# Reciprocal denominators sent through DRAM instead of through TensorE, and a border between two layers put in another order

## The chip, the cores and the metric

The kernel runs on one NeuronCore of a Trainium2 chip. The metric is the device time of one execution in microseconds; the number that counts is the median of several runs.

## What is computed

Four layers over 2048 tokens of width 576: linear attention, MLP, linear attention, MLP, each with a residual. The same weights serve both layers of a kind.

```python
def _A_ref(x, wqkv, wo):                       # 32 heads of 18
    q, k, v = split_heads(x @ wqkv)
    phi = lambda t: jnp.where(t > 0, t + 1, jnp.exp(t)) + 1e-6
    pq, pk = phi(q), phi(k)
    kv  = jnp.einsum("bhsd,bhse->bhde", pk, v)
    z   = jnp.einsum("bhsd->bhd", pk)
    num = jnp.einsum("bhqd,bhde->bhqe", pq, kv)
    den = jnp.einsum("bhqd,bhd->bhq", pq, z)[..., None] + 1e-6
    return merge_heads(num / den) @ wo

def _B_ref(x, w1, b1, w2, b2):                 # 576 -> 4608 -> 576
    h = gelu(_layernorm(x) @ w1 + b1)
    return h @ w2 + b2

x = x + _A_ref(_layernorm(x)); x = x + _B_ref(_layernorm(x))   # twice over
```

The output is x, in bfloat16.

## The kernel before

**Attention.** For each of 16 token tiles of 128 the kernel makes k and v, and adds up `kv` over all tokens in one PSUM pair (`kvacc`). The q products are made in 20 pieces (`q_proj`): five groups of seven heads (126 rows, the last of four heads and 72 rows) times four blocks of 512 tokens. Nine of them stand among the token tiles, eleven in the border. phi(q) of a piece lies in a `units` buffer; its second half on VectorE (`finish`, two instructions) can be done later.

After the last tile, `kv` is multiplied with `wo` once (`kv_wo`), so that the output of a tile of 128 tokens (`wo_stage`) is ten matmuls of 288 columns, five groups by two halves, plus an addition to x on VectorE. Before that, phi(q) has to be divided by the denominators. `den_stage(c)` makes the denominators of one block of 512 tokens in PSUM (32 heads by 128 tokens, four times), takes the reciprocal (`rden`), and lays it out with a mask. `scale_stage(g, c)` then spreads the 32 head rows over the 126 rows of a group with a matmul against a 0/1 matrix (`head_bc`, 512 columns, result in `rden_ps`), and VectorE multiplies phi(q) by it.

**The border.** The MLP's first block needs only the first four token tiles. So the kernel starts its first product while blocks 2 to 4 of the attention are still to be scaled and multiplied out. A first-product group (`m1_group`, four units of 128 hidden rows, 512 tokens) is 36 matmuls that use only 64 rows of TensorE each, upper and lower half side by side, so two run at a time; each half of a unit must finish before the other half begins on the same PSUM bank, and a tiny ScalarE copy (`relay`) carries that order. ScalarE then evicts each unit with gelu; the fourth eviction of a group (`held`) is put behind the next group's relay, or, in the border, flushed at once. Eight groups stand in the border and a ninth in `run`, then the second product (`m_ps`) begins. All instructions of an engine run in the order in which the source issues them (`InOrder`, `pe`).

**PSUM.** Two pairs of banks (`accA`, `accB`) are used in turn by groups, `wo_stage`, `kv_wo` and the second product; four single banks (`one`) go round among everything else. A group takes two singles and one pair: units 0 and 2 lie in the singles, units 1 and 3 in the pair. Evictions go 0, 2, 1, 3.

**The first border, in TensorE's order:** the last q products, `den_stage(0)` and the five scalings of block 1 (three read PSUM directly, two go over a ScalarE copy); four times a `wo_stage` with the next layer's norm, q products and transposes of the norm's output between them, `den_stage(1)` after the second; then

```python
            scales(1, 0, 1); finish(4); group()
            scales(1, 2, 3); finish(1); den_stage(2); group()
            scales(1, 4);    finish(4); group()
            for c in (1, 2, 3):          # wo_stage, one scaling, wo_stage, one scaling, group,
                ...                      # twice per block; den_stage(3) in block c == 1
```

The border of the second attention layer is written by the same code.

Of the kernel before, what the change touches and what calls it, by code (L numbers as in the profile page):

```python
# [15 lines left out]
P = 128  # L16
# [4 lines left out]
G = 5  # L21
# [14 lines left out]
def build(tc, A_x, A_wqkv, A_wo, B_w1, B_b1, B_w2, B_b2, out, n_layers=4):  # L36
    nc = tc.nc
    with ExitStack() as ctx:
# [3 lines left out]
        work = ctx.enter_context(tc.tile_pool(name="work", bufs=2))  # L42

# [124 lines left out]
        relay_sb = const.tile([P, 2], F32, name="relay_sb")  # L168
        pool.memset(relay_sb[:], 0.0)
# [102 lines left out]
        class Norm:  # L272
# [32 lines left out]
            def norm(self):  # L305
# [10 lines left out]
                if self.kind == "B":  # L316
                    pool.tensor_copy(out=y[:, D:DPAD], in_=y[:, 4 * P:D])
# [84 lines left out]
        def layer_A(li, next_kind, begin, before_tile, mid_tile, rows_ahead, after_tile, q_tiles, placed, mlp):  # L402
# [155 lines left out]
            quad_rden, turn = {}, dict(rb=0)  # L558

            def spare(i):  # L560

                return yT[:, i, CA:2 * CA]

            def den_stage(c):
# [9 lines left out]
                quad = spare(3 + c % 2)  # L574
                vec.tensor_tensor(out=quad.rearrange("p (j n) -> p j n", j=4), in0=quad_mask[:],
                                  in1=rden[:].unsqueeze(1).to_broadcast([P, 4, P]), op=ALU.mult)
                quad_rden[c] = quad

            def scale_stage(g, c, direct=False):
                bp = one("rden_ps")  # L580
                mm(bp[:], head_bc[:, g, :], quad_rden[c], True, True)
                if direct:
                    vec.tensor_tensor(out=pq[(g, c)][0:GR[g], 0:CA], in0=bp[0:GR[g], :],
                                      in1=pq[(g, c)][0:GR[g], 0:CA], op=ALU.mult)
                    return
                turn["rb"] += 1
                rb = spare(turn["rb"] % 3)
                act.copy(out=rb[0:GR[g], :], in_=bp[0:GR[g], :])
                vec.tensor_tensor(out=pq[(g, c)][0:GR[g], 0:CA], in0=pq[(g, c)][0:GR[g], 0:CA],
                                  in1=rb[0:GR[g], :], op=ALU.mult)  # L590
# [11 lines left out]
            first = [Norm(t, "B", "act" if t < 3 else "dve", "act" if t < 2 else "dve") for t in range(TPC)]  # L602
# [26 lines left out]
            q_next(True)  # L629
            first[2].transposed()  # L630
            q_next(True)
            first[3].transposed()
            warm_table(ACT.Gelu_apprx_tanh)
# [3 lines left out]
            def scales(c, *groups):  # L637
                for g in groups:
                    scale_stage(g, c, direct=True)

            def group():
                mlp.m1_group(0, mlp.done)
                mlp.flush()

            scales(1, 0, 1)
            finish(4)
            group()
            scales(1, 2, 3)
            finish(1)
            den_stage(2)  # L650
            group()
            scales(1, 4)
            finish(4)
            group()
            for c in (1, 2, 3):
                t = c * TPC
                nxt = scales if c < 3 else lambda *a: None
                wo_stage(t)
                nxt(c + 1, 0)
                wo_stage(t + 1)  # L660
                nxt(c + 1, 1)
                group()
                wo_stage(t + 2)
                nxt(c + 1, 2)
                wo_stage(t + 3)
                nxt(c + 1, 3, 4)
                if c == 1:
                    den_stage(3)
                if c < 3:
                    group()  # L670
# [4 lines left out]
        class LayerB:  # L675
# [4 lines left out]
            def m1_group(self, c, g):  # L680
# [5 lines left out]
                dst = [early[0][:], late[:, 0, :], early[1][:], late[:, 1, :]]  # L686
# [29 lines left out]
                for i, (hi, n, wt, mv) in enumerate(order):  # L716
# [11 lines left out]
                    if seen[n] == 9 and n != 3:  # L728
                        evict(n)
# [8 lines left out]
            def run(self):  # L738
# [6 lines left out]
                for c in range(NCB):  # L745
# [15 lines left out]
                    for j in range(TPC):  # L761
                        t = c * TPC + j
                        acc = pair("m2_ps")
                        if t == NT - 1 and li == n_layers - 1:
                            for half in range(2):
                                cols = slice(half * HALF, (half + 1) * HALF)
                                for f in range(NF):
                                    mm(acc[:, half, 0:HALF], hT[f][:, j * P:(j + 1) * P], w2_sb[:, f, cols],
                                       f == 0, f == NF - 1)
                                vec.tensor_tensor(out=x_sb[:, t, cols], in0=acc[:, half, 0:HALF],  # L770
                                                  in1=xo_of[t][:, cols], op=ALU.add)
                                sp.dma_start(out=out_f[t * P:(t + 1) * P, cols], in_=x_sb[:, t, cols])
                            break
                        for f in range(NF):
# [145 lines left out]
```

## Time and profile before

| | us |
|---|---|
| median of 3 runs | 778.02 (778.01 to 778.48) |
| profiled execution, its own time | 777.94 |
| span of its profile | 776.2 |
| TensorE busy | 767.1 |
| ScalarE busy | 315.8 |
| VectorE busy | 274.3 |

The span is the time between the first and the last instruction; the profiled execution's own time has 1.7 us around it. A row of the timeline reads: start, length, engine, line, operation, output and inputs, shapes, count, and in brackets the idle time before it with what ended it. A row's length for a matmul is longer than the step to the next matmul, since they overlap; steps are read from start times. PE is TensorE, PEld its weight loads, DVE is VectorE, ACT ScalarE, POOL GpSimd, SPq the queue on which SyncE issues DMAs.

### The profile page before, as it was taken

Reading aid. Unit: us, or ns where it says so; the run is one execution under the profiler, and the core shown is the slowest. Engines: PE = TensorE matmul, PEld = TensorE weight load, DVE = VectorE, ACT = ScalarE, POOL = GpSimd, SP = SyncE. Lnnn points to the kernel's source line nnn. Section 1 sums busy time; section 2 is a strip of 40 time slices with the busy share of each in tenths; the row PEclk is TensorE's granted clock in tenths of the full one; section 3 lists DMA queues with packets and bytes.
Section 4 is the critical chain, followed back from the end, with each engine's and each line's share of the span. In section 5 each row is a group of like instructions: output and inputs, shape, how many; then the busy total and the mean of one; then the engine's idle time right before and its main releaser. Section 6 shows DMA issues by size and latency. Waiting matters only on the chain.

```text
span 776.2 us, 15424 instructions
## 1 busy us (share of the span) xinstructions
PE 767.1 (99%) x6559; PEld 488.2 (63%) x6580; DVE 274.3 (35%) x636; ACT 315.8 (41%) x657; POOL 113.1 (15%) x238
## 2 busy tenths in 40 slices
PE   8999999999999999999999999999999999999998
PEld 5776555675477457646777754557745764675476
DVE  7876753435223402400354576443130240100000
ACT  5677744204710660274046586331075027305700
POOL 4540200223112201200200020003120120010010
PEclk9999999999999999999999999999999999999999
DMA  8990000010001101010000000000100100010000
GB/s 210 246 352 12 1 1 2 1 35 24 14 11 25 36 1 35 6 30 3 1 17 19 1 3 1 1 2 21 40 7 1 45 21 2 8 50 10 1 16 16
DMA packets 51086, 25.69 MB, mean 33 GB/s; under 512 B 35146, under 2 KB 51018, under 8 KB 51018
## 3 DMA queue, kind: packets, MB, share of 16 engines
q1 hardware_dynamic: 51018, 24.71, 11.8%
q8 instruction: 51, 0.84, 0.5%
q14 instruction: 17, 0.14, 0.1%
HBM read 15.79 MB, written 2.36 MB: 23 GB/s over the span
## 4 chain that ended last, share of the span: by engine, by line
PE 91%; ACT 4%; DVE 3%; issue 1%; POOL 0%; DMA 0%; DVEq 0%; POOLq 0%
PE m_ps L181 36%; PE h_ps L181 19%; PE hp_ps L181 15%; PE v_ps L181 5%; PE k_ps L181 5%; PE q_ps L181 4%; ACT units L52 3%; PE wo_ps L181 3%; PE kvacc L181 1%; DVE units L52 1%; PE rden_ps L181 1%; DVE x_sb L52 1%; DVE ln_st L52 1%; PE tp L330 1%; PE kvwo_ps L181 0%
## 5 line engine op out<-in xcount | busy, mean ns | idle before, releaser
L181 PEld LDWEIGHTS <-units 128*128 128x128 bf16 (+2 forms) x2624 | 254.5, 98 | 76.6 <-issue 11.7
L181 PE MATMUL m_ps<-w_sb,units 128*128 128x288 bf16 x2304 | 283.8, 286 | 0.6 <-DVE x_sb L52 0.6
L181 PEld LDWEIGHTS <-w_sb 64*128 64x128 bf16 x2304 | 124.6, 94 | 138.1 <-issue 7.7
L181 PE MATMUL hp_ps<-yT,w_sb 64*128 64x512 bf16 x1152 | 175.7, 376 | 0.0
L181 PE MATMUL h_ps<-yT,w_sb 64*128 64x512 bf16 x1152 | 151.1, 376 | 1.0 <-DVE units L52 0.6
L52 ACT COPY relay_sb<-relay_sb 128x1 f32<-128x1 f32 x144 | 27.5, 191 | 289.4 <-PE h_ps L181 268.0
L52 DVE TENSOR_TENSOR x_sb<-m_ps,xo 128x576 bf16<-128x576 f32 (+1 forms) x33 | 24.4, 739 | 323.1 <-PE m_ps L181 323.1
L52 ACT ACTIVATE units<-h_ps,b1T 128x512 bf16<-128x512 f32 x144 | 91.2, 684 | 44.5 <-PE h_ps L181 43.2
L52 POOL TENSOR_TENSOR xo<-x_sb,b_bc 128x576 f32<-128x576 bf16 x32 | 40.8, 1275 | 416.5 <-DVE x_sb L52 298.0
L52 ACT ACTIVATE units<-hp_ps,b1T 128x512 bf16<-128x512 f32 x144 | 96.2, 688 | 0.0
L181 PEld LDWEIGHTS <-yT 128*128 128x128 bf16 x640 | 60.8, 97 | 18.7 <-ACT yT L52 1.1
L181 PE MATMUL h_ps<-yT,w_tail 64*128 64x512 bf16 x144 | 54.1, 376 | 0.0
L181 PE MATMUL hp_ps<-yT,w_tail 64*128 64x512 bf16 x144 | 54.1, 376 | 0.0
L52 DVE BATCH_NORM_STATS2 ln_st<-x_sb 128x6 f32<-128x288 bf16 x128 | 51.2, 441 | 1.3 <-DMA x_sb<-in_A_x_dram 0.9
L52 ACT ACTIVATE units<-q_ps 128x512 bf16<-128x512 f32 x80 | 43.4, 602 | 15.7 <-PE q_ps L181 10.9
L181 PE MATMUL q_ps<-yT,wq_sb 128*128 128x512 bf16 x185 | 47.4, 379 | 0.8
L52 DVE STREAM_TRANSPOSE shared<-y_ring 128x640 bf16<-128x640 bf16 x40 | 33.0, 828 | 42.4 <-DMA yT<-shared 40.7
L181 PE MATMUL wo_ps<-shared,units 126*128 126x288 bf16 (+1 forms) x320 | 44.9, 286 | 1.0
L181 PE MATMUL k_ps<-wkv_sb,yT 128*128 128x288 bf16 x320 | 44.6, 286 | 0.2 <-ACT yT L52 0.2
L181 PE MATMUL v_ps<-wkv_sb,yT 128*128 128x252 bf16 (+1 forms) x320 | 44.6, 285 | 0.0
L52 DVE TENSOR_TENSOR x_sb<-wo_ps,x_sb 128x576 bf16<-128x576 f32 x32 | 24.2, 757 | 52.0 <-PE wo_ps L181 50.9
L52 DVE TENSOR_SCALAR y_ring<-x_sb,ln_mv,ln_rstd 128x576 bf16<-128x576 bf16 x58 | 30.7, 529 | 28.2 <-POOL ln_rstd L52 28.2
(69 smaller groups left out, 401.5 us busy)
## 6 DMA issues: line engine op xcount, KB each, us to landing
yT<-shared SPq DMA_DIRECT2D x160, 40.0 KB, 1.9
w_sb<-in_B_w_dram SPq DMA_DIRECT2D x12, 432.0 KB, 8.5
w_sb<-in_B_w_dram SPq DMA_DIRECT2D x9, 512.0 KB, 9.4
x_sb<-in_A_x_dram SPq DMA_DIRECT2D x16, 144.0 KB, 3.3
out_dram<-x_sb SPq DMA_DIRECT2D x15, 144.0 KB, 1.7
wkv_sb<-in_A_wqkv_dram SPq DMA_DIRECT2D x2, 288.0 KB, 3.3
w_tail<-in_B_w_dram SPq DMA_DIRECT2D x2, 288.0 KB, 11.5
wo_sb<-in_A_wo_dram SPq DMA_DIRECT2D x1, 567.0 KB
```

The lines of the kernel that those rows point to most:

```text
L52: inst = issue(*args, **kw)
L181: return pe(nc.tensor.matmul(out_, lhsT=lhsT, rhs=rhs, start=start, stop=stop, **kw))
L330: pe(nc.tensor.transpose(out=tp[:, k, :], in_=self.y[:, k * P:(k + 1) * P], identity=ident[:]))
```

## The change

1. Block 1 is scaled as before, with all five scalings reading PSUM directly. For blocks 2 to 4, `den_stage` ends with four DMAs that write the reciprocals to DRAM as 32 rows of 512, and `spread(c)` reads them back with five DMAs, each head's row 18 times over, into a free part of `yT` (`spare(g)`). `scale_stage` then multiplies two buffers of SBUF on VectorE, without a matmul.
2. The border is written in another order: groups stand in runs of 3, 2, 2 and 1 (the ninth follows the last), with the four `wo_stage` of a block together between them. All nine late finishes come before the first group. `den_stage(1)` moves behind the last transpose. In the first part, a q product goes between the third and fourth scaling, and the norms, q products and transposes are rearranged.
3. In a group, units 0 and 2 lie in the pair and units 1 and 3 in the singles; the eviction of unit 0 is issued when both 0 and 2 are complete. The order of evictions is the same, 0, 2, 1, 3.
4. The last tile's second product takes a single bank for each half instead of one pair. The copies of three transposes instead of two go to VectorE, and so does the small tail copy of the norm of tile 3.

```diff
+        dpool = ctx.enter_context(tc.tile_pool(name="dram", bufs=1, space=DRAM))
...
+        rden_rows = [dpool.tile([H, CA], BF16, name=f"rden_rows{c}") for c in range(NCA)]
...
             def den_stage(c):
...
-                rden = work.tile([P, P], BF16, name="rden", bufs=1)
+                rden = work.tile([P, P], BF16, name="rden", bufs=2)
                     vec.reciprocal(out=rden[:], in_=dp[:, 0:P])
+                if c > 0:
+                    for j in range(TPC):
+                        sp.dma_start(out=rden_rows[c][:, j * P:(j + 1) * P], in_=rden[32 * j:32 * (j + 1), :])
+                    return
...
+            def spread(c):
+                for g in range(G):
+                    sp.dma_start(out=spare(g)[0:GR[g], :],
+                                 in_=rden_rows[c][7 * g:7 * g + GH[g], :].unsqueeze(1).to_broadcast([GH[g], DH, CA]))
+
+            def scale_stage(g, c):
+                rows = slice(0, GR[g])
+                if c > 0:
+                    by = spare(g)
+                else:
+                    by = one("rden_ps")
+                    mm(by[:], head_bc[:, g, :], quad_rden, True, True)
+                vec.tensor_tensor(out=pq[(g, c)][rows, :], in0=by[rows, :], in1=pq[(g, c)][rows, :], op=ALU.mult)
...
-            for g in range(G):
-                if g == 3:
-                    kv_wo(4, act)
-                scale_stage(g, 0, direct=g < 3)
+            for g in range(3):
+                scale_stage(g, 0)
+            kv_wo(4, act)
+            q_next(True)
+            scale_stage(3, 0)
+            scale_stage(4, 0)
             q_next(True)
             for t in range(TPC):
                 wo_stage(t)
-                if t >= 1:
+                if t in (1, 2):
                     first[t - 1].norm()
                 first[t].stats()
                 first[t].rstd()
-                q_next(True)
-                if t >= 2:
-                    first[t - 2].transposed()
-                if t == 1:
-                    den_stage(1)
+                if t < 2:
+                    q_next(True)
+                if t == 2:
+                    first[0].transposed()
+            q_next(True)
+            first[2].norm()
+            first[1].transposed()
+            q_next(True)
+            q_next(True)
             first[3].norm()
...
             first[2].transposed()
             first[3].transposed()
+            den_stage(1)
+            spread(1)
             warm_table(ACT.Gelu_apprx_tanh)
...
+            def groups(n):
+                for _ in range(n):
+                    mlp.m1_group(0, mlp.done)
+                    mlp.flush()
...
+            finish(9)
+            scales(1)
+            groups(3)
+            for t in range(TPC, 2 * TPC):
+                wo_stage(t)
+                if t < TPC + 2:
+                    den_stage(t - 2)
+            spread(2)
+            scales(2)
+            spread(3)
+            groups(2)
+            outputs(2)
+            scales(3)
+            groups(2)
+            outputs(3)
+            groups(1)
...
-                dst = [early[0][:], late[:, 0, :], early[1][:], late[:, 1, :]]
+                dst = [late[:, 0, :], early[0][:], late[:, 1, :], early[1][:]]
...
-                    if seen[n] == 9 and n != 3:
-                        evict(n)
+                    if n in (0, 2) and seen[0] == seen[2] == 9:
+                        evict(0)
+                        evict(2)
+                    if n == 1 and seen[1] == 9:
+                        evict(1)
...
                         if t == NT - 1 and li == n_layers - 1:
                             for half in range(2):
                                 cols = slice(half * HALF, (half + 1) * HALF)
+                                acc = one("m2_ps")
                                 for f in range(NF):
-                                    mm(acc[:, half, 0:HALF], hT[f][:, j * P:(j + 1) * P], w2_sb[:, f, cols],
+                                    mm(acc[:, 0:HALF], hT[f][:, j * P:(j + 1) * P], w2_sb[:, f, cols],
                                        f == 0, f == NF - 1)
```

More of the change, by code (lines that the diff above doesn't have):

```diff
@@ L316, in norm @@
                 if self.kind == "B":
-                    pool.tensor_copy(out=y[:, D:DPAD], in_=y[:, 4 * P:D])
+                    (vec if self.eng == "dve" and self.transpose != "dma" else pool).tensor_copy(out=y[:, D:DPAD], in_=y[:, 4 * P:D])
             def transposed(self):
@@ L599, in wo_stage @@
                 residual(li, t, wp[:, :, 0:HALF])
-            first = [Norm(t, "B", "act" if t < 3 else "dve", "act" if t < 2 else "dve") for t in range(TPC)]
+            first = [Norm(t, "B", "act" if t < 3 else "dve", "act" if t == 0 else "dve") for t in range(TPC)]
             finish(1)
@@ L648, in layer_A, with scales @@
[L648 to L657, printed above, removed]
-                wo_stage(t)
[L659 to L670, printed above, removed]
+            def scales(c):
+                for g in range(G):
+                    scale_stage(g, c)
@@ L773, in run @@
                             break
+                        acc = pair("m2_ps")
                         for f in range(NF):
```

34 lines of the change are left out of this document (5 added, 29 removed).

## Prediction, made before the changed kernel was run

> **What bounds the kernel now.** First the page: busy shares, the granted clock, the chain that ended last.
>
> ```profile
> PE 767.1 (99%) x6559; PEld 488.2 (63%) x6580; DVE 274.3 (35%) x636; ACT 315.8 (41%) x657; POOL 113.1 (15%) x238
> ...
> PEclk9999999999999999999999999999999999999999
> ...
> PE 91%; ACT 4%; DVE 3%; issue 1%; POOL 0%; DMA 0%; DVEq 0%; POOLq 0%
> ```
>
> TensorE is the bound and its clock is whole, so time comes only out of matmuls that go away and of stretches in which TensorE holds an instruction back. A busy share of 99% hides such stretches, because the ends of matmuls are modelled; they are found by start times against paces. The chain of waits gives the paces, from stretches in which nothing disturbs:
>
> ```profile
> 66.48 1.08 PE q_ps L181 x5
> ...
> 93.26 0.40 PE den_ps L181 x20
> ...
> 145.45 35.39 PE m_ps L181 x288
> ...
> 184.83 1.08 PE h_ps L181 x9
> 188.71 1.08 PE h_ps L181 x9
> ...
> 446.51 1.08 PE q_ps L181 x5
> ...
> 525.48 35.39 PE m_ps L181 x288
> ```
>
> A matmul of 512 columns takes 1.08/5 = 0.216 us, one of 288 columns 35.39/288 = 0.123 (so the ten of a `wo_stage` 1.23), a `den_stage` 0.40, and a first-product group in a row of such groups 188.71 - 184.83 = 3.88. The q product at 66.48 and the second product at 145.45 come again at 446.51 and 525.48, both 380.03 us later: the border of the second attention layer is that of the first over again, and what holds for one is counted twice.
>
> Then the timeline of the first border, TensorE's rows and two that bear on them:
>
> ```profile
> 71.34 0.81 PE L181 MATMUL rden_ps<-yT,head_bc 128*128 128x512 bf16 x3
> ...
> 84.31 0.44 PE L330 MATMUL tp<-ident,y_ring 128*128 128x128 bf16 x5
> ...
> 84.59 1.24 PE L181 MATMUL q_ps<-yT,wq_sb 128*128 128x512 bf16 x5
> ...
> 87.49 0.59 PE L181 MATMUL rden_ps<-yT,head_bc 128*128 128x512 bf16 x2
> 87.69 0.49 DVE L52 COPY yT<-tp 128x640 bf16<-128x640 bf16 x1 [0.51 <-PE tp L330]
> ...
> 88.23 1.46 PE L181 MATMUL h_ps<-yT,w_sb 64*128 64x512 bf16 x8
> ...
> 92.65 0.60 PE L181 MATMUL rden_ps<-yT,head_bc 128*128 128x512 bf16 x2
> ...
> 97.80 0.39 PE L181 MATMUL rden_ps<-yT,head_bc 128*128 128x512 bf16 x1
> ...
> 98.12 1.04 PE L181 MATMUL h_ps<-yT,w_sb 64*128 64x512 bf16 x8
> ...
> 108.18 1.26 ACT L52 ACTIVATE units<-h_ps,b1T 128x512 bf16<-128x512 f32 x2 [0.62 <-PE h_ps L181]
> ...
> 109.14 2.89 PE L181 MATMUL wo_ps<-shared,units 126*128 126x288 bf16 x20
> ...
> 112.80 0.39 PE L181 MATMUL h_ps<-yT,w_sb 64*128 64x512 bf16 x1
> 113.48 1.02 PE L181 MATMUL h_ps<-yT,w_sb 64*128 64x512 bf16 x7 [0.29 <-DVE units L52]
> ...
> 117.46 1.41 PE L181 MATMUL wo_ps<-shared,units 126*128 126x288 bf16 x10
> ...
> 131.75 2.90 PE L181 MATMUL wo_ps<-shared,units 126*128 126x288 bf16 x20
> ...
> 134.57 1.04 PE L181 MATMUL h_ps<-yT,w_sb 64*128 64x512 bf16 x8
> ...
> 138.56 2.89 PE L181 MATMUL wo_ps<-shared,units 126*128 126x288 bf16 x20
> ...
> 141.39 1.04 PE L181 MATMUL h_ps<-yT,w_sb 64*128 64x512 bf16 x8
> ...
> 145.38 4.83 PE L181 MATMUL m_ps<-w_sb,units 128*128 128x288 bf16 x38
> ```
>
> I split the border at 87.49, where the last transpose has left TensorE. From there to the second product at 145.38 lie 57.89 us. Work by paces: nine groups 34.92, twelve `wo_stage` 14.76, fifteen spreading matmuls (`rden_ps`) 3.24, two `den_stage` 0.80: 53.72. So 4.2 us are lost, and the rows say where. A group that stands alone costs more than 3.88: from the spreading matmul at 97.80 to the group at 98.12 there are 0.32 where 0.216 would do, and the group from 141.39 to 145.38 takes 3.99: 0.1 to enter and 0.1 to leave the row-tiled state, nine times: 1.8. The first group takes 92.65 - 88.23 = 4.42, 0.43 over 3.99, and begins 0.2 after its turn, for VectorE's copy of the last transpose at 87.69: 0.6. The one at 112.80 takes 4.66, held by VectorE's scaling: 0.7. Two `wo_stage` at 131.75 and 138.56 take 2.82 and 2.83 to the next group where 2.46 + 0.1 would do, 0.26 each; the pair of banks is still being emptied. That is 3.6 of 4.2; the rest is scattered.
>
> **The change, part by part.**
>
> *Spreading matmuls.* Blocks 2 to 4 lose 15 matmuls of 0.216: 3.2 per layer.
>
> *Groups left undisturbed.* The runs of groups become 3, 2, 2 and 2 (the eighth, and the ninth that always followed): four entries and exits instead of nine, 5 x 0.2 = 1.0. Against it: each group is flushed at its end, so its fourth eviction stands ahead of the next group's relay on ScalarE. Two evictions in a row take 1.26 (the row at 108.18), so four end some 2.5 us after the first begins. That is 0.9 before its group ends (109.14 less 0.1, against 108.18); the next group's second halves need the relay half a group in, 1.94 after that end, so 2.8 after the first eviction began. It is just enough: 0 to 0.2 for each of five joints, and I take 0.
>
> *Bank order.* Units 0 and 2, evicted first, now lie in the pair, so the pair is free for `wo_stage` about 1.2 us earlier, more than the 0.26 that it was late. With the scalings no longer between groups the waits at 112.80 go too. The first group's wait stays in part: it needs the copy of the last transpose, about 0.7 after that leaves TensorE, and only `den_stage(1)` of 0.4, moved there, fills it: 0.3.
>
> Second part after: 34.92 + 4 x 0.2 + 14.76 + three `den_stage` 1.20 + 0.3 = 52.0, against 57.89: 5.9 less.
>
> *First part, 71.34 to 87.49.* 16.15 us hold five spreading matmuls 1.08, two `kvwo` 0.25, seven q products 7.56, four `wo_stage` 4.92, `den_stage(1)` 0.40, and four transposes of 84.59 - 84.31 = 0.28: 15.33, so 0.8 is lost. The change takes `den_stage` out (0.4) and puts a q product between the third and fourth scaling, which leaves VectorE room; scaling straight out of PSUM replaces a ScalarE copy and a VectorE product. Between none and all of the 0.8 goes; I take half, 0.4. Together 0.8. One transpose more, and the tail of tile 3's norm, go to VectorE, beside q products.
>
> *The end.* The last tile's second half waits for the first half's addition, since both lie in one pair; now each half has a bank of its own:
>
> ```profile
> 768.45 4.57 PE L181 MATMUL m_ps<-w_sb,units 128*128 128x288 bf16 x36 [0.62 <-DVE x_sb L52]
> ```
>
> 0.6 less, once. The steady groups of blocks 2 to 4 evict in the same order at the same times and keep 3.88.
>
> Sum: 2 x (5.9 + 0.8) + 0.6 = 14.0. The profiled execution took 777.94 (span 776.2 and 1.7 around it), 0.08 under the median 778.02; 777.94 - 14.0 = 763.9, and the difference to the median is below what I resolve.
>
> **What must be hidden.** The scaling of a block now waits for DMA: four writes to DRAM, then five reads that depend on them, all on SP. Nothing in the trace does this, so I bound it:
>
> ```profile
> out_dram<-x_sb SPq DMA_DIRECT2D x15, 144.0 KB, 1.7
> ...
> L52 SPq DMA_DIRECT2D yT<-shared x16: 586/602/1165, 186.2 to 196.6; - x16
> ...
> L52 SPq DMA_DIRECT2D x_sb<-in_A_x_dram x16: 384/431/1613, 0.8 to 18.2; - x16
> ...
> DMA to landing us min/median/max: 2.2/3.3/3.8
> ...
> DMA packets 1925, 2.13 MB, mean 354 GB/s; under 512 B 79, under 2 KB 1925, under 8 KB 1925
> ```
>
> and VectorE's part of the chain, from the groups by form:
>
> ```profile
> L52 DVE TENSOR_TENSOR x_sb<-wo_ps,x_sb 128x576 bf16<-128x576 f32 x32 | 24.2, 757 | 52.0 <-PE wo_ps L181 50.9
> ...
> L52 DVE TENSOR_TENSOR units<-units 128x512 bf16<-128x512 bf16 x40 | 17.0, 426 | 3.8 <-DVE units L52 0.5 <-ACT units L52 0.4
> ...
> L52 DVE TENSOR_SCALAR units<-units 128x512 bf16<-128x512 bf16 x40 | 12.1, 301 | 0.8 <-ACT units L52 0.8
> ...
> L52 DVE RECIPROCAL rden<-den_ps 128x128 bf16<-128x128 f32 x8 | 7.5, 939 | 1.1 <-PE den_ps L181 1.1
> ```
>
> A write lands 1.7 us after issue (stores of the output), a read 2.2 at best (loads of x), a write's issue takes about 0.4. Let s be the time by which each read follows the one before. Its floor is the issue, 0.43 to 0.60. Its ceiling is all 126 rows on one of 16 DMA engines: at 354/16 = 22 GB/s (the loads of the second weight, 46 to 52 us) a row of 1024 bytes takes 0.046, 126 of them 5.8. I take 0.6, by the yT row, whose transfers have the most pieces.
> [...]
>
> Count from the start of the first group. The reciprocal ends at about 0.8, the last write lands at 3.75, the reads are issued from 3.8 and land from 6.0 to 6.0 + 4s, and the last scaling (0.43, VectorE) ends at 6.4 + 4s; the first product that uses it stands at 12.45, after three groups: there is time while s is under 1.5. VectorE first does nine finishes (9 x 0.73 = 6.6), ready at 7.4, ahead of the scaling and not behind it (a finish is 0.301 + 0.426). Block 3: `wo_stage` 4 ends at 13.2, then addition 0.76 and reciprocal 0.94 on VectorE; reads wait on SP behind the writes of block 4 as well, to 18.3, and land up to 20.5 + 4s, 0.43 before they are scaled; needed at 26.2: s under 1.3. Block 4: its reads wait till block 3's scalings have read the buffer, and are needed at 39.1: s under 2.0. Queued behind a late scaling on VectorE are only additions of later `wo_stage`; on SP only later spreads.
>
> **Rivals.** (1) Reads somewhat late: s from 1.3 to 2.2. Above 1.5 a layer loses what blocks 2 and 3 come late by, (4s - 6.05) + (4s - 5.3) = 8s - 11.35; at 1.8, 3.05, twice, so 770.0. For it: nothing in the trace reads the same DRAM row 18 times. Against: at 0.6, or twice that, nothing is lost. (2) Slower: the spread transfers land on too few DMA engines. It decides where that loss eats the gain of a layer, 8s - 11.35 = 6.7, at s = 2.26. On two engines s = 63 x 0.046 = 2.9; then block 4's chain governs, 20.9 + 9s + (4s - 6.05) against 39.1, a loss of 13.4 a layer: 763.9 + 26.9 = 790.8. For it: seven source heads are an odd number to share out. Against: it takes fewer than three of 16. (3) Joints stall 0.2 each: 10 x 0.2 = 2.0, so 765.9.
>
> **How the numbers follow.** Forecast 763.9, with the undecided terms (first part 0 to 0.8 a layer, joints 0 to 2.0, the scattered rest) from 761.5 to 766.5, rival 3 in it: 0.77. Rival 1: 0.12. Rival 2: 0.09. Something between, near 778: 0.02. The range 761.5 to 771 takes the forecast and the cheaper part of rival 1. A measurement tells 0.2%, 1.6 us, from no change: faster 0.88, same 0.02, slower 0.10.
>
> **What would show it.** In the profile after: no `rden_ps` beyond the five of each layer's block 1; groups 3.88 apart in runs of 3, 2, 2 and 2; `m_ps` about 6.7 us earlier; PE rows of `wo_ps` after a run waiting for nothing. Wrong it is if `wo_ps` or its weight load waits for VectorE's `units` or that for `yT<-rden_rows`: then the reads' landing times, and their spacing s above all, say which rival. If the runs of groups have a period over 3.95, the joints stall.

## The result, and the profile after

The changed kernel takes 764.38 us (median of four runs, 764.16 to 765.92) against 778.01 before in the same comparison (four runs, 778.00 to 778.48): a ratio of 0.9828, 95% interval 0.9811 to 0.9845, so 13.6 us or 1.7% less. The forecast was 763.9. The profiled execution took 764.59, with a span of 762.9.

From the page of the kernel after, the rows that answer to the first ones shown of before:

```profile
PE 756.7 (99%) x6550; PEld 485.9 (64%) x6550; DVE 267.1 (35%) x634; ACT 311.7 (41%) x651; POOL 112.5 (15%) x236
...
PEclk9999999999999999999999999999999999999999
...
PE 97%; DVE 1%; DMA 1%; SPq 0%; POOL 0%; issue 0%
```

TensorE is busy 10.4 us less, at the same clock. The chain that ended last now runs over TensorE for 97% of the span, where ScalarE and VectorE had 7% of it. The new DMA path has less than 1% of it: the page names the load of x at the start (`x_sb<-in_A_x_dram`) as its 1% of DMA.

The chain of waits of after, at the places by which the borders were measured before:

```profile
66.83 1.08 PE q_ps L183 x5
...
139.52 5.50 PE m_ps L183 x44
```

```profile
440.57 1.08 PE q_ps L183 x5
...
473.33 1.34 PE wo_ps L183 x10
...
513.07 6.97 PE m_ps L183 x56
```

From the q product to the second product the first border takes 72.69 us and the second 72.50, where both took 78.97: 6.28 and 6.47 less: the second product comes earlier by nearly the 6.7 that the forecast had. The rest of the 13.3 us between the two spans is 0.9 behind the second border (from 513.07 to the end of the span 249.8, from 525.48 before 250.7), less 0.35 by which the q product of the first layer starts later (66.83 against 66.48), ahead of anything that the change touches.

TensorE's rows of the first border, from the timeline:

```profile
71.69 0.81 PE L183 MATMUL rden_ps<-yT,head_bc 128*128 128x512 bf16 x3
...
86.99 0.47 PE L183 MATMUL den_ps<-units,zsel 127*32 127x128 bf16 x20
...
87.76 1.04 PE L183 MATMUL hp_ps<-yT,w_sb 64*128 64x512 bf16 x8 [0.30 <-DVE yT L53]
...
99.52 1.41 PE L183 MATMUL wo_ps<-shared,units 126*128 126x288 bf16 x10
...
113.44 5.29 PE L183 MATMUL wo_ps<-shared,units 126*128 126x288 bf16 x40
...
118.66 1.04 PE L183 MATMUL hp_ps<-yT,w_sb 64*128 64x512 bf16 x8
...
126.54 5.10 PE L183 MATMUL wo_ps<-shared,units 126*128 126x288 bf16 x40
...
139.45 6.79 PE L183 MATMUL m_ps<-w_sb,units 128*128 128x288 bf16 x54
```

Three groups lie between 87.76 and 99.52, 11.76 us: three times 3.88 and 0.12 at the end of the run. Between 118.66 and 126.54 lie two, 7.88, which is two times 3.88 and the same 0.12. No joint stalls, and the first group waits 0.30, as forecast. The four `wo_stage` of block 4 follow one another in 131.57 - 126.54 = 5.03 (the next group starts at 131.57), those of block 3 in 118.66 - 113.44 = 5.22. That 0.19 is the only place where the DMA path holds TensorE up, and SP's and VectorE's rows say how:

```profile
88.60 3.06 SPq L53 DMA_DIRECT2D rden_rows<-rden  x4
92.82 4.13 SPq L53 DMA_DIRECT2D yT<-rden_rows  x5
102.61 3.89 SPq L53 DMA_DIRECT2D rden_rows<-rden  x8
106.67 8.25 SPq L53 DMA_DIRECT2D yT<-rden_rows  x10
```

```profile
95.86 0.43 DVE L53 TENSOR_TENSOR units<-yT,units 126x512 bf16<-126x512 bf16 x1 [0.74 <-DMA yT<-rden_rows]
...
99.48 0.42 DVE L53 TENSOR_TENSOR units<-yT,units 72x512 bf16<-72x512 bf16 x1 [0.31 <-DMA yT<-rden_rows]
...
109.78 0.43 DVE L53 TENSOR_TENSOR units<-yT,units 126x512 bf16<-126x512 bf16 x1 [3.36 <-DMA yT<-rden_rows]
...
113.64 0.42 DVE L53 TENSOR_TENSOR units<-yT,units 72x512 bf16<-72x512 bf16 x1 [0.36 <-DMA yT<-rden_rows]
```

Each first row of a block is the first scaling, each second the last. A scaling starts when its read has landed. The last scaling is needed by the fifth matmul of the block's first `wo_stage`, 4 x 0.123 = 0.49 after that stage's start: at 100.01 for block 2, at 113.93 for block 3. It ends at 99.90 and at 114.06. So block 2 is in time by 0.1 us and block 3 late by 0.1, where the forecast saw 3.6 and 2.9 us to spare. In the second layer block 2 has 1.4 us to spare (its last scaling ends at 472.33 and is needed at 473.75) and block 3 again 0.1 (487.57 and 487.66); block 4 is scaled by 121.19, 5 us ahead of its stage at 126.54. The gain is the one forecast; the margin under it is almost gone.

### The profile page after: what moved, and what is told of

Its sections match the earlier page's. It is cut to its first block, busy times and chain, and to the rows that moved or that the text cites. A ratio compares the mean times of both kernels' runs of the same rounds, so it can differ in the third digit from the quotient of the medians.

```text
span 762.9 us, 15463 instructions
## 1 busy us (share of the span) xinstructions
PE 756.7 (99%) x6550; PEld 485.9 (64%) x6550; DVE 267.1 (35%) x634; ACT 311.7 (41%) x651; POOL 112.5 (15%) x236
## 4 chain that ended last, share of the span: by engine, by line
PE 97%; DVE 1%; DMA 1%; SPq 0%; POOL 0%; issue 0%
PE m_ps L183 37%; PE hp_ps L183 20%; PE h_ps L183 16%; PE q_ps L183 6%; PE wo_ps L183 5%; PE v_ps L183 5%; PE k_ps L183 5%; PE kvacc L183 1%; PE tp L332 1%; DMA x_sb<-in_A_x_dram 1%; SPq L53 0%; PE den_ps L183 0%; PE kvwo_ps L183 0%; DVE yT L53 0%; DVE ln_st L53 0%; DVE units L53 0%
## 5 line engine op out<-in xcount | busy, mean ns | idle before, releaser
L183 PE MATMUL h_ps<-yT,w_sb 64*128 64x512 bf16 x1152 | 177.8, 376 | 0.0
L183 PE MATMUL hp_ps<-yT,w_sb 64*128 64x512 bf16 x1152 | 148.2, 376 | 0.6 <-DVE yT L53 0.6
L53 ACT ACTIVATE units<-hp_ps,b1T 128x512 bf16<-128x512 f32 x144 | 91.2, 684 | 58.8 <-PE hp_ps L183 58.8
L53 ACT ACTIVATE units<-h_ps,b1T 128x512 bf16<-128x512 f32 x144 | 96.2, 688 | 0.0
L183 PE MATMUL q_ps<-yT,wq_sb 128*128 128x512 bf16 x200 | 49.4, 379 | 0.2
L183 PE MATMUL wo_ps<-shared,units 126*128 126x288 bf16 (+1 forms) x320 | 42.6, 286 | 0.0
L53 ACT ACTIVATE phi_e<-k_ps 128x288 bf16<-128x288 f32 x64 | 24.6, 418 | 38.5 <-PE k_ps L183 36.8
```

The lines of the kernel that those rows point to most:

```text
L53: inst = issue(*args, **kw)
L183: return pe(nc.tensor.matmul(out_, lhsT=lhsT, rhs=rhs, start=start, stop=stop, **kw))
```

## The experiments

**Theory:** the parts add up. The spreading matmuls are worth their own time, each group that no longer stands alone 0.2, the banks and the tail the waits they end; the DMA path costs nothing as long as its reads are in time. **Rivals:** the order alone carries the gain and the path through DRAM little; the path through DRAM does what the spread on TensorE did, at a price that is hidden only by luck; the transfers' time is set not by the number of DMA engines but by their issue.

### The parts, one by one

The kernel before with the new banks and the last tile's single banks alone:

```diff
-                dst = [early[0][:], late[:, 0, :], early[1][:], late[:, 1, :]]
+                dst = [late[:, 0, :], early[0][:], late[:, 1, :], early[1][:]]
...    # and the eviction condition and the last tile's second product, as in the change
```

> Kernel before with only the new bank order and the single banks of the last tile. Theory 1: the last tile's 0.6 us, two waits of 0.26 us a layer ahead of output tiles, and the smaller ones of 0.08 (four a layer): 778.0 - 0.6 - 2 x 0.8 = 775.8 (774.5 to 777). Theory 2, the bank order needs the runs to be of use: only the 0.6, 777.4.

Measured: 774.64 (774.54 to 774.65), ratio 0.9956 (0.9939 to 0.9972), 3.4 us less than before. By the chains of waits its two borders take 77.72 and 77.71 us where before takes 78.97, 1.25 less each, and 0.7 go behind the second border. The forecast had named only two waits for the pair of banks, 0.26 each, but the timeline of before has one at five of the six pairs of output stages. The first of them:

```profile
102.11 2.90 PE L181 MATMUL wo_ps<-shared,units 126*128 126x288 bf16 x20
...
104.84 0.38 PE L181 MATMUL rden_ps<-yT,head_bc 128*128 128x512 bf16 x1
```

These twenty matmuls take 2.73 where 2.46 would do; only the pair at 117.46 has no such wait.

The order, banks and tail of after, but the spread of blocks 2 to 4 on TensorE; block 2's five spreads stand ahead of the first run of groups, those of blocks 3 and 4 between the output stages:

```diff
             def scale_stage(g, c):
-                if c > 0:
-                    by = spare(g)
-                else:
-                    by = one("rden_ps")
-                    mm(by[:], head_bc[:, g, :], quad_rden, True, True)
+                by = one("rden_ps")
+                mm(by[:], head_bc[:, g, :], quad_of[c], True, True)
...
-            finish(9)
             scales(1)
+            finish(9)
```

> Changed kernel with the reciprocals of blocks 2 to 4 spread by TensorE again (15 matmuls a layer, VectorE scaling out of PSUM), in the new order with its runs of groups: block 2's five ahead of the first group, block 3's and 4's between and behind the output tiles. Theory 1, the DMA is what makes the order worth it: 15 x 0.216 = 3.2 us of matmuls a layer come back, and TensorE waits for the four single banks, which VectorE empties at 0.6 us each, two or three us more a layer: 764.4 + 11 = 775 (773 to 777). Theory 2, the order and the bank order bring the gain and the spreading hides either way: at most the matmuls themselves, 764.4 + 6.5 = 771 or less.

Measured: 775.40 (775.26 to 775.74), ratio 0.9967 (0.9954 to 0.9980). That is 0.8 us slower than the banks and the tail alone: with the spread on TensorE the new order loses. The timeline shows the place, here in the first layer:

```profile
87.22 0.47 PE L182 MATMUL den_ps<-units,zsel 127*32 127x128 bf16 x20
89.32 1.55 PE L182 MATMUL rden_ps<-yT,head_bc 128*128 128x512 bf16 x5 [1.63 <-DVE yT L53]
```

If the first run of groups is to stay whole, the spreads of block 2 stand ahead of it, right behind their denominators, and TensorE has to stand still for the reciprocal and the mask on VectorE. In the old order output stages, q products and transposes stand between the two. The second layer has the same 1.63 once more. With the 6.5 us of matmuls, the two stretches (after waits 0.30 there) account for 9.1 of the 11.0 us between this kernel and after.

The kernel before with only the spread of blocks 2 to 4 sent through DRAM, old order, old banks, old tail:

```diff
+                if c > 0:
+                    for j in range(TPC):
+                        sp.dma_start(out=rden_rows[c][:, j * P:(j + 1) * P], in_=rden[32 * j:32 * (j + 1), :])
+                    return
...
             scales(1, 4)
+            spread(2)
             finish(4)
```

> The kernel before with only the way of the spread changed: blocks 2 to 4 go through DRAM (writes behind the reciprocals, reads issued at the place where the first scaling of the block stood), while the order of the border, the nine runs of groups, the bank order and the last tile stay as before. Theory 1 (three parts that add: spreading matmuls, runs and joints, banks and tail): only the 15 spreading matmuls of each layer go, 15 x 0.216 us = 3.2 us a layer, 6.5 us in all, and of the waits that stood at those matmuls a little: 771 us (770 to 772.5). Theory 2 (the new order is what makes the path through DRAM bearable: the old one asks for the scaled units sooner than the data come): the first group behind the spread of each block waits for the reads, 1 us or more per block, six blocks: 776 us or more. Theory 3 (the way through DRAM carries the whole gain, the order nothing): 766 us or less.

Measured: 770.61 (770.14 to 770.89), ratio 0.9906 (0.9889 to 0.9922): theory 1. Of the 7.3 us, 6.5 are the thirty matmuls. The rest is a balance: the wait in the group at 112.80 is gone, the first group takes 4.03 instead of 4.42, and the second and the third group now stand together; against that the pair of banks is waited for at all six pairs of output stages instead of five.

The same with the new banks and the tail:

```diff
-                dst = [early[0][:], late[:, 0, :], early[1][:], late[:, 1, :]]
+                dst = [late[:, 0, :], early[0][:], late[:, 1, :], early[1][:]]
...
+                                acc = one("m2_ps")
```

> The kernel before with the spread of blocks 2 to 4 through DRAM, the new bank order and the last tile's single banks, but the old order of the border with its nine runs of groups. What remains to the kernel after is the order alone. Theory 1 (spread, banks and order add up): against the run with the old banks (770.6 us), the six pairs of output stages of a layer fall from 2.89 to 2.64 us, 1.5 us a layer, and the tail by 0.6: 3.6 us less, 767.0 us (766.5 to 768), and the order is then worth 2.6 us, near 1 us a layer for five joints at 0.2 us plus the first part. Theory 2 (the banks' waits are only hidden behind the DMA spread's other slack): 769 us or more. Theory 3 (the order is worth nothing once the spread goes through DRAM): 764.4 to 765.5 us.

Measured: 766.58 (766.31 to 766.68), ratio 0.9851 (0.9834 to 0.9867). From the timelines of these two, the first pair of output stages without and with the banks:

```profile
100.20 2.89 PE L183 MATMUL wo_ps<-shared,units 126*128 126x288 bf16 x20
```

```profile
100.54 2.64 PE L183 MATMUL wo_ps<-shared,units 126*128 126x288 bf16 x20
```

Six pairs by 0.25 by two layers are 3.0, and with 0.7 for the tail the 4.0 between the two medians is nearly told (3.5 between the two profiled executions, 770.14 and 766.68). What is left to the kernel after, 766.58 - 764.38 = 2.2 us, is the order. Its parts are read from where the first group and the second product start in this run:

```profile
88.23 1.04 PE L183 MATMUL hp_ps<-yT,w_sb 64*128 64x512 bf16 x8 [0.58 <-DVE yT L53]
...
140.31 5.93 PE L183 MATMUL m_ps<-w_sb,units 128*128 128x288 bf16 x47
```

Between these two lie 52.08 us, against 139.45 - 87.76 = 51.69 in after; in the second layer 52.07 against 51.50. So the runs of groups are worth 0.4 and 0.6. The old order has eight runs of groups once the scalings have left TensorE, the new one four: four joints at 0.2 are 0.8, less 0.2 for two `wo_stage` that now stand ahead of a `den_stage` (1.34 instead of 1.23), and in the first layer less the 0.19 of the late read. The other 0.65 of each layer lie ahead of the first group, in the rearranged first part and the shorter wait for the last transpose (0.30 instead of 0.58). The parts add up to 2.3 us.

After with the old banks:

```diff
-                dst = [late[:, 0, :], early[0][:], late[:, 1, :], early[1][:]]
+                dst = [early[0][:], late[:, 0, :], early[1][:], late[:, 1, :]]
```

> Changed kernel with the old bank order: units 0 and 2 in single banks, 1 and 3 in the pair. Theory 1: an output tile needs the pair of the last group only as second of four, 1.2 us behind the run's end, when the last eviction is nearly done; 0 to 0.3 us late at each of three places a layer, 764.4 + 0.6 (764.4 to 766.2). Theory 2, the bank order carries a good part of the gain: the 0.26 to 0.3 us waits of the kernel before come back at all places, and with fewer places no more than 2 us: 766.

Measured: 765.65 (765.47 to 765.89), ratio 0.9841 (0.9826 to 0.9855), 1.3 more than after. Two rows of its timeline:

```profile
114.44 4.61 PE L183 MATMUL wo_ps<-shared,units 72*128 72x288 bf16 x36 [0.39 <-DVE units L53]
...
126.86 5.36 PE L183 MATMUL wo_ps<-shared,units 126*128 126x288 bf16 x40
```

The stages of block 4 wait for the pair of banks again, 5.36 against 5.10 (in the second layer those of block 3 do so too), and at block 3 of the first layer the wait falls together with a late read that is longer than after's. So the bank order still pays with runs of groups, but with fewer places to pay at than the six pairs of the old order.

After with the runs of groups split again for blocks 3 and 4, from 3, 2, 2, 2 into 3, 2, 1, 1, 1, 1:

```diff
-            outputs(2)
+            wo_stage(8)
+            wo_stage(9)
+            groups(1)
+            wo_stage(10)
+            wo_stage(11)
             scales(3)
-            groups(2)
-            outputs(3)
             groups(1)
+            wo_stage(12)
...
```

> Changed kernel with the runs of groups 3, 2, 1, 1, 1, 1 instead of 3, 2, 2, 2 (an output pair of tiles between two groups, as before the change). Theory 1: two more entries and exits a layer at 0.2 us, and no waits with the new bank order: 764.4 + 0.8 = 765.2. Theory 2, the run length itself does not matter: 764.4.

Measured: 765.18 (765.00 to 765.53), ratio 0.9835 (0.9820 to 0.9850): 0.8 more than after, two entries and exits of 0.2 in each of two layers, as expected. The intervals of the two ratios overlap, but the borders agree with the medians: the second takes 72.92 us instead of 72.50, and the first 72.92 instead of 72.69, where the late read's 0.19 of after is missing.

Together, in medians:

| spread | order | banks, tail | us |
|---|---|---|---|
| TensorE | old | old | 778.02 |
| TensorE | old | new | 774.64 |
| TensorE | new | new | 775.40 |
| DRAM | old | old | 770.61 |
| DRAM | old | new | 766.58 |
| DRAM | new | new | 764.38 |

With the new banks the path through DRAM is worth 8.1 us in the old order and 11.0 in the new one; the order is worth 2.2 with it and costs 0.8 without, in the placement tried here; another placement of the spreads was not run. The first rival falls by the third row, and so does the simple sum: order and spread are one part, not two.

### What the reads cost

Each kernel here is after with another shape of the reads: k rows of DRAM, each repeated to fill the same number of partitions (128 and 80 instead of 126 and 72 with sixteen). With two, three and sixteen rows the scalings so take other heads' denominators; only the time is of use.

```diff
-                     sp.dma_start(out=spare(g)[0:GR[g], :],
-                                  in_=rden_rows[c][7 * g:7 * g + GH[g], :].unsqueeze(1).to_broadcast([GH[g], DH, CA]))
+                    copies = GR[g] // 2                     # 3; with 16 rows: 8, and 5 for the last group
+                    sp.dma_start(out=spare(g)[0:2 * copies, :],
+                                 in_=rden_rows[c][0:2, :].unsqueeze(1).to_broadcast([2, copies, CA]))
```

Two rows:

> Changed kernel; each read takes 2 rows of the reciprocals 63 times (36 for the small group) instead of 7 rows 18 times, the same bytes and descriptors. The scaling so uses other heads' denominators. Theory 1, the number of DMA engines that a read gets divides the outer size: 2 engines, 63 rows x 0.046 us, so the reads follow each other by s = 2.9 us. With the landing seen in the changed profile (first read used 8.1 us after the first group began, needed at 12.3), block 2 comes about 7.9 us late in the first layer and 6.4 in the second, and blocks 3 and 4, whose reads queue up, 9.2 more in each: 764.4 + 33 = 797, slower than the kernel before. Theory 2, the engines do not hang on the number of heads: s stays near 0.78 and the time at 764.4.

Three rows:

> As reads_2 with 3 rows 42 times (24 for the small group). Theory 1: 3 engines, s = 42 x 0.046 = 1.93; late by 4.0 and 2.5 us (block 2 of the two layers) and 3.9 in each (block 3), 14.3 together: 778.7, about the kernel before. Theory 2: 764.4.

Sixteen rows:

> As reads_2 with 16 rows 8 times (5 for the small group), 128 rows. Theory 1: 16 engines, so only the issue limits and s falls from 0.78 to between 0.45 and 0.73; the 0.2 us that block 3 came late in the first layer goes: 764.0 to 764.4. Theory 2: s stays near 0.78, 764.4.

Measured: two rows 800.13 (799.94 to 800.32), ratio 1.0284 (1.0263 to 1.0305); three rows 779.03 (777.66 to 782.37), ratio 1.0024 (1.0007 to 1.0042); sixteen rows 764.09 (764.07 to 764.57), ratio 0.9822 (0.9808 to 0.9837). Scalings follow the landings. Two rows, from VectorE's timeline, and the DMA view of 98 to 104 us (packets, MB, share of 16 engines):

```profile
97.05 0.43 DVE L53 TENSOR_TENSOR units<-yT,units 126x512 bf16<-126x512 bf16 x1 [2.15 <-DMA yT<-rden_rows]
99.72 0.43 DVE L53 TENSOR_TENSOR units<-yT,units 126x512 bf16<-126x512 bf16 x1 [2.25 <-DMA yT<-rden_rows]
```

```profile
q1 hardware_dynamic: 286, 0.29, 13.6%
```

Three rows, the timeline and the DMA view of 95 to 99 us:

```profile
96.28 0.43 DVE L53 TENSOR_TENSOR units<-yT,units 126x512 bf16<-126x512 bf16 x1 [1.47 <-DMA yT<-rden_rows]
98.06 0.42 DVE L53 TENSOR_TENSOR units<-yT,units 126x512 bf16<-126x512 bf16 x1 [1.36 <-DMA yT<-rden_rows]
```

```profile
q1 hardware_dynamic: 289, 0.29, 20.4%
```

For comparison the same row of before while the second weight is loaded at 354 GB/s (46 to 52 us):

```profile
q1 hardware_dynamic: 1925, 2.13, 108.0%
```

The spacing s is 2.67 us with two rows at 48 GB/s, and 1.78 with three at 72: 24 GB/s for each row, and k times s is 5.34 in both. Where all 16 engines are at work the share reads 108.0%, so 13.6% and 20.4% are 2.0 and 3.0 engines. So in these two runs as many engines are at work as there are rows, and an engine needs 5.34 / 126 = 0.042 us for a row of 1024 bytes. Its 24 GB/s are no less than the 354 / 16 = 22 of the weight load: reading one row over and over costs nothing extra here, which answers what the prediction's first rival had for it. By the same product seven rows would have an estimated 5.34 / 7 = 0.76, and in the second layer of after the scalings of block 2 follow one another in 0.72 to 0.77. Theory 1 of the expectations was an assumption of the author's; the runs show it for two and three rows, with 2 x 24 and 3 x 24 GB/s.

With 14 source rows and the whole computation the rows can be written twice and read nine times each:

```diff
-        rden_rows = [dpool.tile([H, CA], BF16, name=f"rden_rows{c}") for c in range(NCA)]
+        rden_rows = [dpool.tile([H, 2, CA], BF16, name=f"rden_rows{c}") for c in range(NCA)]
...
-                                 in_=rden_rows[c][7 * g:7 * g + GH[g], :].unsqueeze(1).to_broadcast([GH[g], DH, CA]))
+                                 in_=twice[14 * g:14 * g + 2 * GH[g], :].unsqueeze(1).to_broadcast([2 * GH[g], DH // 2, CA]))
```

> Changed kernel, with each head's row written twice to DRAM (64 rows) and read 9 times, so that a read has 14 source rows. The computation is whole. Theory 1: 14 engines (8 in the small group), s from 0.78 down to the issue, 0.45 to 0.73; the reads land about 1 us earlier at the end of a block; time 764.0 to 764.4, because they were hidden but for 0.2. Theory 2: s 0.78 and 764.4, or more if the doubled writes cost issue time.

Measured: 765.22 (764.90 to 765.55), ratio 0.9835 (0.9821 to 0.9850): 0.8 more than after. That is outside the range of theory 1; theory 2 had left it open, for doubled writes that cost issue time. The view of one tile's instructions (count: least, median, longest ns) says why, first for 14 rows, then for after, then for 16:

```profile
L53 SPq DMA_DIRECT2D yT<-rden_rows x30: 667/795/1301, 93.0 to 490.2; - x30
L53 SPq DMA_DIRECT2D rden_rows<-rden x24: 550/593/1062, 88.6 to 481.1; - x24
```

```profile
L53 SPq DMA_DIRECT2D yT<-rden_rows x30: 642/733/907, 92.8 to 487.7; - x30
L53 SPq DMA_DIRECT2D rden_rows<-rden x24: 307/419/1744, 88.6 to 479.5; - x24
```

```profile
L53 SPq DMA_DIRECT2D yT<-rden_rows x30: 521/556/1242, 92.5 to 486.6; - x30
```

With 14 rows the transfers reach 338 and 348 GB/s within the first two reads of block 3, about 14 times 24, and fall to 0 between them (DMA view, 108 to 112 us): SP's issue becomes the pace, 0.795 us a read, no faster than the 0.76 of seven rows. Each doubled write takes 0.593 instead of 0.419, so that the reads of block 3 leave later (108.24 instead of 106.67). Sixteen rows take 0.556 to issue and would have settled the margin (in that run the last scaling of block 3 ends at 112.06 and is needed at 114.10), but this reference has 32 heads in groups of seven. So the engines set the pace with two and three rows (2.67 and 1.78 us) and the issue with 14 (0.795), and with seven the two are nearly equal (an estimated 0.76 and a measured 0.733): the theory holds below that, its rival above.

### Taking the late read away

After with the writes of block 4 issued behind the reads of block 3:

> The kernel after with the four writes of block 4 issued behind the five reads of block 3 on SP's queue instead of ahead of them; nothing else differs. Theory 1 (SP's issues are what makes the last read of block 3 late by 0.2 us a layer, and DMA is nowhere else on the path): the reads of block 3 start 4 issues sooner, about 1.7 to 2 us, the stage of tiles 8 to 11 falls from 5.3 to about 5.0 us, and the time is 764.4 less 0.2 to 0.4 us: 764.0 to 764.2 us, with block 4's data still more than 4 us early. Theory 2 (the late read is set by the transfers themselves): no change, 764.4 us.

Measured: 764.05 (764.04 to 764.56), ratio 0.9822 (0.9807 to 0.9837). The median lies in the range of theory 1, but the step it forecast did not happen:

```profile
102.28 2.16 SPq L53 DMA_DIRECT2D rden_rows<-rden  x4
106.40 3.83 SPq L53 DMA_DIRECT2D yT<-rden_rows  x5
```

```profile
114.08 1.16 PE L183 MATMUL wo_ps<-shared,units 72*128 72x288 bf16 x8 [0.32 <-DVE units L53]
```

The reads wait 106.40 - 104.44 = 1.96 us for the landing of their own writes; the four other writes had only filled that time. The late read is as late as before. What sets the start of the reads in this layer is not SP's order but the landing of the writes ahead of them. In the second layer nothing had been late: the stages of block 3 take 5.04 us there in both kernels. The transfers have a part as well: in both kernels one read of block 3 lands some 0.7 us later behind its neighbour than the others (from 109.78 to 111.34 in after, from 111.30 to 112.85 here), and without that the last scaling would have been in time. What holds this one read up the profile does not show. The 0.3 between the medians is within what the first layer's start varies by (66.49 here, 66.83 in the profile of after, for the same q product), so no gain is claimed.

That left the chain itself. After with the denominators of blocks 3 and 4 ahead of the output stages:

```diff
             for t in range(TPC, 2 * TPC):
-                wo_stage(t)
                 if t < TPC + 2:
                     den_stage(t - 2)
+                wo_stage(t)
```

> The kernel after with the denominators of blocks 3 and 4 computed ahead of the output stages of tiles 4 and 5 instead of behind them: reciprocal, writes and reads of block 3 move ahead by one output stage (about 1.4 us), and the first output stage of block 2 stands 0.5 us later, which the scaled units of block 2 have as a margin. Theory 1 (the late read of block 3 is set by the chain reciprocal, write, landing, read, which starts at the denominators): the wait of 0.26 us in the stage of tile 8 goes, the stage of tiles 8 to 11 falls from 5.2 to about 5.0 us, and the time is 764.1 us (763.9 to 764.3). Theory 2 (the late read is set by the transfers of five reads at 0.8 us each, wherever they start): unchanged, 764.4 us.

Measured: 763.90 (763.79 to 764.05), ratio 0.9818 (0.9803 to 0.9832). The timelines of SP, VectorE and TensorE:

```profile
105.18 7.98 SPq L53 DMA_DIRECT2D yT<-rden_rows  x10
```

```profile
111.70 0.42 DVE L53 TENSOR_TENSOR units<-yT,units 72x512 bf16<-72x512 bf16 x1 [0.48 <-DMA yT<-rden_rows]
```

```profile
113.02 5.11 PE L183 MATMUL wo_ps<-shared,units 126*128 126x288 bf16 x40
```

and the chain of waits:

```profile
66.52 1.08 PE q_ps L183 x5
...
138.92 6.11 PE m_ps L183 x49
```

The reads leave at 105.18 instead of 106.67, the last scaling ends at 112.12, 1.4 us before its matmul at 113.51, and the stages of block 3 take 118.06 - 113.02 = 5.04 like those of block 4 (the next group starts at 118.06). The border takes 72.40 instead of 72.69: 0.19 is the late read, and 0.1 comes from one `wo_stage` less ahead of a `den_stage`, which the second layer shows alone (72.40 instead of 72.50). Theory 1 holds in the trace. It is the lowest median of all the kernels; against after the 0.5 us lies within the intervals of the two ratios, and what the borders show for it is 0.3 in the first layer and 0.1 in the second.

## Why the prediction came out right

**Spreading matmuls, 3.2 a layer.** Right: 7.3 us for the spread alone, 6.5 of them by matmuls.

**Groups left undisturbed, 1.0 a layer, joints at no cost.** Right: groups 3.88 apart, and 0.8 us for two joints put back in each of the two layers. Rival 3 is out. Of the five joints one went already with the scalings; the order brings the other four. What the prediction had not seen is that the order pays only with the spread off TensorE: with it there the new order, as placed here, loses 0.8.

**Banks.** The waits were counted at two places by 0.26; before has them at five of its six pairs. The three further waits are 0.8, about the 0.6 that the prediction called scattered. The sum held because it was made from paces, all work at its own speed, and not from the waits that had been named.

**Second part of the border, 52.0.** 139.45 - 86.99 = 52.46 in the first layer. Of the 0.46, 0.19 is the late read, and 0.2 are two entries and exits that the sum left out: a `wo_stage` ahead of a `den_stage` takes 1.34 instead of 1.23, twice (the chain's row at 473.33 is one of the two in the second layer). The first part fell by 16.15 - (86.99 - 71.69) = 0.85, forecast 0.8, though half of that forecast was a choice in the middle of a range. The tail gave 0.7 rather than 0.6 by the run with the banks and the tail alone; another 0.2 behind the second border has no cause that the runs show.

**What must be hidden: right in its outcome, wrong in its sizes.** This is the step that was nearly lost. From the start of the first group, for block 2 of the first layer:

| | forecast | measured |
|---|---|---|
| issue of the four writes | 1.6 | 3.06 (1.73 in the second layer) |
| reads issued from | 3.8 | 5.06 |
| issue to first landing | 2.2 | 3.04 |
| spacing s | 0.6 | 0.91 (0.75 in the second layer) |
| last scaling ends | 8.8 | 12.14 |
| needed at | 12.45 | 12.25 |

Each size was taken from the nearest row and each was low; together they used 3.5 of the 3.6 us to spare. That they did not use more is luck: nothing in the sum had tied them to that bound. For s the nearest row was the wrong one to follow: 0.6 is the issue time of another transfer (`yT<-shared`), while seven rows issue in 0.73 and by the product above move in 0.76. With an s of 0.76 the forecast would still have been 763.9.

**Rivals 1 and 2.** Priced too low by the same sizes. By the prediction's formula, s = 1.8 would leave 770.0 and break even would come at 2.26; the run with s = 1.78 stood at 779.03, at break-even already, and the run with 2.67 at 800.13. The expectation for the first of these, which took the landing from the profile of after, came to 778.7, so it is the sizes that were wrong. The mechanism of the slower case, too few engines, was right (2.0 at work with two rows), its threshold was not, and the kernel stands at 0.91, not at 0.6, on the way to it.

## What to carry to other kernels

Work that TensorE does only to copy rows can be moved to DMA if its result is needed a few groups later. Count the whole chain (reciprocal, write issue, landing, read issue, landing, scaling) with some 7 us from the first write's issue to the scaling by the first landed read (88.60 to 95.86 here, and 476.35 to 483.11 in the second layer), and start it as early as its input allows: in the first layer, moving the denominators by one stage bought the margin that twice the rows and another queue order did not. Sum a stretch from paces and subtract it from what it takes, since named waits are never all of them.

## What the runs showed of the hardware

**TensorE's clock after a stall.** The run with two rows lay 3 us above its expectation, and a lower clock accounts for at least part of that. The table by stretches of that kernel (length, busy of PE, PEld, DVE, ACT, POOL, then the granted clock, DMA share and GB/s) and TensorE's timeline:

```profile
99.50:105.50 6.00, 0.82 (x3) 0.20 (x2) 1.27 (x3) 1.45 (x3) 0.00 (x0) 0.71 0.14 48
105.50:112.00 6.50, 5.35 (x49) 2.85 (x53) 2.16 (x4) 0.00 (x0) 0.00 (x0) 0.50 0.04 10
```

```profile
109.28 2.58 PE L183 MATMUL wo_ps<-shared,units 126*128 126x288 bf16 x10
111.79 0.69 PE L183 MATMUL den_ps<-units,zsel 127*32 127x128 bf16 x20
```

After a stretch in which TensorE mostly waited (busy for 0.82 of 6.00 us), its clock is granted at 0.50, and ten matmuls take 2.51 us up to the next instruction instead of 1.34. So the late transfer is paid twice here: by the wait, and by slow matmuls behind it. How much waiting brings the clock down no run here measures. No single wait of that stretch is longer than 2.37 us, with one matmul between two waits, so the clock fell here without TensorE standing still in one piece. In the run with three rows, whose waits were shorter (1.46 at most), the clock was still granted at 1.00 while TensorE waited, and fell to 0.59 behind that:

```profile
99.00:103.00 4.00, 1.23 (x8) 0.30 (x4) 1.23 (x3) 1.86 (x4) 0.00 (x0) 1.00 0.16 57
103.00:107.20 4.20, 4.09 (x36) 2.34 (x36) 1.68 (x3) 0.00 (x0) 0.00 (x0) 0.59 0.02 4
```

**Issue time differed with the shape.** A read of some 126 KB takes SP 0.556 us with 16 rows, 0.733 with seven and 0.795 with 14, and single writes of 32 rows by 256 bytes took from 0.307 to 1.744.
